# Rows of kv added by accumulating DMAs, and an order of work that knows of a port shared by VectorE and POOL

## The chip, the cores and the metric

The kernel runs on one core of one Trainium2 chip. Five engines work side by side on that core, each through its own instructions in a fixed order: TensorE (PE, with its weight loads PEld), VectorE (DVE), ScalarE (ACT), GpSimd (POOL) and SyncE (SP, which here only issues DMAs). POOL issues DMAs too. The metric is the time of one execution on the device, in microseconds (us). Three executions of the kernel before took 2118.57, 2122.62 and 2124.64 us, so the median is 2122.62 us.

## The reference

Two parts run one after the other. The first is attention over pooled keys: `kv` (4 batches, 384 x 32 x 128) is averaged over blocks of 4 x 4, multiplied by `w_sr`, and is both key and value for `q` (4 batches of 12288 rows of 128). The second is a mixture of 8 experts: each of the 49152 result rows goes to its best expert.

```python
kv_pool = kv.reshape(B, H // r, r, W // r, r, C).mean(axis=(2, 4))      # r = 4
k = v = kv_pool.reshape(B, -1, C) @ w_sr                                 # 768 keys per batch
a = softmax((q @ k.transpose(0, 2, 1)) / sqrt(C))
x = (a @ v).reshape(-1, C)
logits = (x / |x|) @ (emb / |emb|).T / tau ;  e = argmax(logits) ;  gate = softmax(logits)[e]
out = gate * (relu(x @ w1[e]) @ w2[e])                                   # F = 1024
```

Everything is float32 outside; the kernel splits its matmul operands into two float16 parts, a high one and a low one.

## The kernel before

The rows of `q` are cut into 96 steps of 512 rows, 24 to a batch. In a step, PE makes the scores `s` (four tiles of 128 x 768, line 668), DVE takes each row's maximum (`nm`, line 673), ACT makes the exponentials `p` (line 691) and their high half `phi` (line 709), DVE or POOL the low half `plo` (line 719), two DMA transposes turn both (line 743), and PE multiplies by the values (`xp`, line 764). POOL splits the result rows (`rows`, line 797) and scatters them to their experts' places in DRAM (line 188, one indirect DMA for 128 rows). A group of four steps has one router chain of small DVE instructions (tiles `n..z`, `y`, `x`, `d`, lines 823 to 960).

From step 23 on, tiles of 512 rows of one expert run between the steps: PE makes `ph` (line 1381), ACT `hh` (line 1388), DVE `hl` (line 1393), PE `po` (line 1417), DVE `o` (line 1427), and POOL scatters it to the output (line 188). After the last step expert tiles run alone.

The pooled keys of batch 0 are made at the start by DVE. Those of batches 1 to 3 are made while the batch before runs, in eight parts of 512 columns. For each part SP loads two tiles `kvt` with two of the four rows each (line 365; two buffers, 384 KB each). POOL adds each pair of rows (line 374), adds the two sums (line 378), and then adds the columns four to one in two instructions, `kvc` (line 390) and `pooled` (line 395). Later PE turns `pooled` (`pp`, line 353), and the keys `k` follow.

The order on each engine is worked out when the kernel is built. Every piece of work is recorded with `add(engine, duration, key, function, *what it waits for)`, and `Plan.run` replays the recording against an assumed clock: the engine that is free first takes, of its pieces that are ready by then, the one with the lowest key. The function is called at that moment, so the instructions of an engine stand in the order in which the plan started them. On the chip each engine runs its own list in that order and waits where a semaphore says so. A piece that is planned at the wrong moment therefore holds up all that stands behind it on its engine. The plan knows engines, DMAs and PSUM banks, and no other resource.

Lines that the change touches: `Op`, `Plan.add`, `Plan.chain` and `Plan.run` (202 to 335), `kv_load`, `kv_rows` and `kv_cols` (361 to 400), `kv_ops` (1502 to 1565), and the places where DVE and POOL work is recorded (1606 to 1791).

Of the kernel before, what the change touches and what calls it, by code (L numbers as in the profile page):

```python
# [51 lines left out]
def attention_moe(  # L52
# [149 lines left out]
    class Op:  # L202


        def __init__(self, eng, dur, key, fn, deps, dma, take, free, hold, lands, stage):
            self.eng, self.dur, self.key, self.fn, self.dma = eng, dur, key, fn, dma
            self.take, self.free, self.lands, self.stage = take, free, lands, stage
            self.left, self.users, self.ready, self.end = 0, [], 0.0, None
            if hold:
                self.ready = key + X["start"] - X["early"]  # L210
            for d in set(deps):
                if d is not None:
                    self.left += 1
                    d.users.append(self)

    class Plan:
# [8 lines left out]
        def add(self, eng, dur, key, fn, *deps, dma=None, take=None, free=None, hold=False, lands=False):  # L225
            op = Op(eng, dur, key, fn, deps, dma, take, free, hold, lands, self.stage)
# [3 lines left out]
        def chain(self, key, step, fns, *deps, dur=0.17, eng="DVE"):  # L230

            ops = []
            for i, fn in enumerate(fns):
                ops.append(self.add(eng, dur, key + i * step, fn, *(deps if not ops else ops[-1:])))
# [15 lines left out]
        def run(self, begin):  # L250

            soon, now, free = {}, {}, {}
            n = stage = 0
# [14 lines left out]
            while any(count):  # L268
# [92 lines left out]
    def kv_load(b, h, i):  # L361
# [4 lines left out]
        st[b]["kvt", h, i] = t  # L366

    def kv_rows(b, h, eng):


        def half(i):
            t = st[b].pop(("kvt", h, i))
            st[b]["r", h, i] = kvs.tile([NI, QC], F32, tag=f"kva{i}", name=f"kva{b}_{h}_{i}", bufs=2)
            eng.tensor_tensor(out=st[b]["r", h, i], in0=t[:, 0, :], in1=t[:, 1, :], op=ALU.add)

        def both():
            r = st[b]["r", h, 0]
            eng.tensor_tensor(out=r, in0=r, in1=st[b].pop(("r", h, 1)), op=ALU.add)

        return [lambda: half(0), lambda: half(1), both]  # L380

    def kv_cols(b, h, eng):


        def third():
            if h == 0:
                st[b]["pooled"] = kvs.tile([NI, NJ, C], F32, tag="pooled", name=f"pooled{b}")
            v = st[b].pop(("r", h, 0)).rearrange("p (j r c) -> p j r c", j=JQ, r=R)
            a3 = kvs.tile([NI, JQ, 2, C], F32, tag="kva3", name=f"kvc{b}_{h}", bufs=2)
            eng.tensor_tensor(out=a3, in0=v[:, :, 0:2, :], in1=v[:, :, 2:4, :], op=ALU.add)  # L390
            st[b]["a", h] = a3

        def fourth():
            a3 = st[b].pop(("a", h))
            eng.tensor_tensor(
                out=st[b]["pooled"][:, h * JQ : (h + 1) * JQ, :], in0=a3[:, :, 0, :], in1=a3[:, :, 1, :],
# [1077 lines left out]
    def kv_rows_0():  # L1474
# [3 lines left out]
        for h in range(NQR // 2):  # L1478
            t0, acc = -46.0 + 4 * h, []
            for i in range(R):  # L1480
# [3 lines left out]
                else:  # L1484
                    if h == 0 and i == R - 1:
                        x_set = setup(-30.0, x_wsr, x_tau, x_emb, acc[-1])
                    acc.append(add("DVE", 1.1, t0 + 1.0 + i, lambda h=h, i=i: kv_sum_0(h, i), first, o, *acc[-1:]))
# [14 lines left out]
    def kv_ops(b):  # L1502
        mine = [None] * NQR
        for h in range(NQR if b else 0):
            t0 = slot(b * SPB, -8 * (X["kv"] - h * X["kvs"]))
            eng, what, ta, tb_ = nc.gpsimd, "POOL", 1.25, 0.7
            rows = kv_rows(b, h, eng)
            parts = []
            for i in range(2):
                o = add("SP", 0.45, t0 + i, lambda h=h, i=i: kv_load(b, h, i), *turn("kvt", 2), dma=1.3, hold=True)  # L1510
# [392 lines left out]
```

## Time and profile before

| | us | share of the span |
|---|---|---|
| median of three executions | 2122.62 | |
| profiled execution, its own time | 2131.34 | |
| its span, first to last instruction | 2129.6 | 100% |
| PE busy | 1953.8 | 92% |
| DVE busy | 1740.2 | 82% |
| ACT busy | 1550.0 | 73% |
| POOL busy | 1329.7 | 62% |

The profiled execution took 8.7 us longer than the median of the other three. Busy time is the time in which an engine had an instruction running; an instruction that has started and is held up inside counts as busy. "Idle" before an instruction is what the engine stood still, with what ended it. The granted TensorE clock is given as a share of full speed (2.4 GHz), and was 0.982 on the mean of the span.

### The profile page before, as it was taken

Reading aid. Unit: us, or ns where it says so; the run is one execution under the profiler, and the core shown is the slowest. Engines: PE = TensorE matmul, PEld = TensorE weight load, DVE = VectorE, ACT = ScalarE, POOL = GpSimd, SP = SyncE. Lnnn points to the kernel's source line nnn. Section 1 sums busy time; section 2 is a strip of 40 time slices with the busy share of each in tenths; the row PEclk is TensorE's granted clock in tenths of the full one; section 3 lists DMA queues with packets and bytes.
Section 4 is the critical chain, followed back from the end, with each engine's and each line's share of the span. In section 5 each row is a group of like instructions: output and inputs, shape, how many; then the busy total and the mean of one; then the engine's idle time right before and its main releaser. Section 6 shows DMA issues by size and latency. Waiting matters only on the chain. (4 is left out here: it accounts for less than half of the span.)

```text
span 2129.6 us, 57497 instructions
## 1 busy us (share of the span) xinstructions
PE 1953.8 (92%) x21396; PEld 1498.0 (70%) x21396; DVE 1740.2 (82%) x3679; ACT 1550.0 (73%) x3256; POOL 1329.7 (62%) x1824
## 2 busy tenths in 40 slices
PE   3787788899989999899999999999999999999998
PEld 1575666677767767677677777777777777777697
DVE  6899788788898897788888888888888888766565
ACT  3888779778767777677777887888888887744443
POOL 1556765377768668477676576566566567567433
PEclk9999999999999999999999999999999999999999
DMA  8897646999879989879887888988888887623242
GB/s 234 195 219 179 170 97 143 170 178 181 163 139 177 163 161 182 175 135 181 156 163 141 148 158 153 198 146 159 149 164 150 149 148 151 116 62 80 57 92 77
DMA packets 844925, 322.64 MB, mean 151 GB/s; under 512 B 793042, under 2 KB 804443, under 8 KB 842848
## 3 DMA queue, kind: packets, MB, share of 16 engines
q1 hardware_dynamic: 817568, 264.13, 66.5%
q0 software_dynamic: 24704, 53.53, 9.6%
q8 instruction: 170, 2.79, 0.5%
q10 hardware_dynamic: 2368, 1.25, 0.2%
q14 instruction: 115, 0.94, 0.1%
HBM read 170.55 MB, written 64.50 MB: 110 GB/s over the span
## 5 line engine op out<-in xcount | busy, mean ns | idle before, releaser
L1393 DVE SCALAR_TENSOR_TENSOR hl<-ph,hh 128x512 f16<-128x512 f32 x740 | 506.7, 685 | 171.2 <-ACT hh L1388 163.9
L1381 PE MATMUL ph<-x,wbuf 128*128 128x512 f16 (+1 forms) x2328 | 606.0, 372 | 24.0 <-DVE hl L1393 23.2
L188 POOL DMA_INDIRECT out_dram<-o,m x388 | 409.0, 1054 | 326.5 <-DVE o L1427 97.7
L1388 ACT ACTIVATE hh<-ph 128x512 f16<-128x512 f32 x740 | 440.7, 596 | 229.6 <-PE ph L1381 176.4
L188 POOL DMA_INDIRECT xs_rows<-rows,pi x384 | 418.7, 1090 | 130.2 <-issue 112.1
L1417 PE MATMUL po<-wbuf,hh 128*128 128x128 f16 x5920 | 453.9, 220 | 34.3 <-ACT hh L1388 22.2
L668 PE MATMUL s<-k,qT 128*128 128x512 f16 (+1 forms) x2304 | 439.6, 330 | 20.3 <-ACT p L691 12.1
L691 ACT ACTIVATE p<-s,nm,qa 128x768 f32<-128x768 f32 x384 | 380.8, 993 | 106.3 <-DVE nm L685 90.3
L1417 PEld LDWEIGHTS <-hh 128*128 128x128 f16 x6208 | 384.0, 98 | 57.1 <-ACT hh L1388 26.5
L719 DVE TENSOR_TENSOR plo<-p,phi 128x768 f16<-128x768 f32 x339 | 344.0, 1016 | 55.0 <-ACT phi L709 45.7
L673 DVE TENSOR_REDUCE nm<-s 128x1 f32<-128x768 f32 x384 | 364.1, 949 | 12.8 <-PE s L668 9.6
L1381 PEld LDWEIGHTS <-wbuf 128*128 128x128 f16 x2544 | 227.1, 98 | 143.3 <-issue 31.1
L668 PEld LDWEIGHTS <-qT 128*128 128x128 f16 x2304 | 217.9, 99 | 149.8 <-issue 30.0
L764 PE MATMUL xp<-v,pthi 128*128 128x137 f16 x4200 | 313.8, 224 | 10.0 <-DVE w L551 4.3
L764 PEld LDWEIGHTS <-pthi 128*128 128x128 f16 x4200 | 275.7, 98 | 48.2 <-issue 13.8
L1417 PEld LDWEIGHTS <-hl 128*128 128x128 f16 x3104 | 230.3, 98 | 112.3 <-issue 3.5
L709 ACT CAST phi<-p 128x768 f16<-128x768 f32 x345 | 287.4, 834 | 11.6 <-DMA pthi<-phi 7.0
L1417 PE MATMUL po<-wbuf,hl 128*128 128x128 f16 x2960 | 287.5, 220 | 0.0
L764 PE MATMUL xp<-v,ptlo 128*128 128x137 f16 x2100 | 188.4, 225 | 2.7 <-DMA ptlo<-plo 2.7
L764 PEld LDWEIGHTS <-ptlo 128*128 128x128 f16 x2100 | 143.0, 98 | 3.2 <-DMA ptlo<-plo 3.2
L797 POOL TENSOR_TENSOR rows<-x,rows 128x512 f16<-128x512 f32 x96 | 114.7, 1195 | 30.2 <-ACT rows L792 29.9
L683 ACT ACTIVATE nm<-nm,scales,qa 128x1 f32<-128x1 f32 x206 | 79.4, 385 | 74.0 <-DVE nm L673 72.3
(359 smaller groups left out, 2042.8 us busy)
## 6 DMA issues: line engine op xcount, KB each, us to landing
wbuf<-w_prep SPq DMA_DIRECT2D x106, 1026.0 KB
kvt<-in_kv_dram SPq DMA_DIRECT2D x64, 384.0 KB
q<-in_q_dram SPq DMA_DIRECT2D x96, 256.0 KB
wf<-in_moe_w_dram SPq DMA_DIRECT2D x16, 512.0 KB
out_dram<-o,m POOLq DMA_INDIRECT x388
xs_rows<-rows,pi POOLq DMA_INDIRECT x384
w_prep<-wo SPq DMA_DIRECT2D x8, 514.0 KB
w_prep<-wo SPq DMA_DIRECT2D x8, 512.0 KB
```

Source lines behind the costliest of these rows:

```text
L188: ins = nc.gpsimd.indirect_dma_start(out=dst[:, :], out_offset=bass.IndirectOffsetOnAxis(ap=idx, axis=0), in_=src, in_offset=None, bounds_ ...
L668: nc.tensor.matmul(t[:, lo:hi], qs[:, l, :], r[:, lo:hi], start=i == 0, stop=i == 2)
L673: V.tensor_reduce(out=nm, in_=ks[k]["s", j], axis=AX.X, op=ALU.max, negate=True)
L691: nc.scalar.activation(out=p, in_=ks[k].pop(("s", j)), func=AF.Exp, bias=ks[k].pop(("nm", j)), scale=ks[k]["fac"],)
L709: nc.scalar.copy(out=hi, in_=p)
L719: eng.tensor_tensor(out=lo, in0=ks[k].pop(("p", j)), in1=hi, op=ALU.subtract)
L764: nc.tensor.matmul(ks[k]["xp", h][:, i, :w], l[:, c, :], r[:, c, :w], start=n == 0, stop=n == len(terms) - 1)
L797: nc.gpsimd.tensor_tensor(out=r[:, :, HP : HP + C], in0=ks[k]["x"][:, :, 0:C], in1=r[:, :, 0:C], op=ALU.subtract)
L1381: nc.tensor.matmul(ph[:, kk * n : (kk + 1) * n], wt[:, o + f : o + f + P], r, start=i == 0, stop=i == 2)
L1388: nc.scalar.activation(out=hh, in_=ts[t]["ph", u], func=AF.Relu)
L1393: V.scalar_tensor_tensor(out=hl, in0=ts[t].pop(("ph", u)), scalar=0.0, in1=ts[t]["hh", u], op0=ALU.max, op1=ALU.subtract)
L1417: nc.tensor.matmul(ts[t]["po"][:, j * C : (j + 1) * C], h[:, kk * n + j * P : kk * n + (j + 1) * P], wt[:, f : f + P], start=u == 0 and i ...
```

## The change

Batches 1 to 3 get their rows of `kv` added by DMA. A tile `kva` now holds 1024 columns (four parts to a batch and four buffers). SP loads the first of the four rows, and POOL issues three DMAs that each add the next row onto the tile, each of which waits until the one before it has landed (`lands=True`, and the chain through `o`). POOL then adds the columns in two instructions, in place and without `kvc`. So a batch has 4 loads and 12 accumulating DMAs where it had 16 loads, and 8 POOL additions where it had 40.

Second, a piece of work can be marked `port=True`. `Plan.run` keeps the time until which DVE and POOL each hold the port by its own reckoning. Where a marked piece would start while the other engine still holds it, the engine takes the lowest-keyed unmarked piece that is ready instead, and where there is none, the piece is reckoned to start when the other engine lets go. Marked are DVE's `plo`, `q_lo`, `w_lo`, the low half of `k`, the router chain and one of the placing steps, and POOL's `rows`, `w_lo`, `plo`, column additions and selection of tiles. The instructions of these pieces stay what they were; the recorded duration of a router step goes from 0.17 to 0.22.

```diff
+            held = dict(DVE=0.0, POOL=0.0)
...
+                if op.port:
+                    other = held["POOL" if eng == "DVE" else "DVE"]
+                    if other > t + 0.1:
+                        rest = [x for x in now[eng] if not x[2].port and self.can_go(x[2])]
+                        if rest:
+                            x = min(rest)
+                            now[eng].remove(x)
+                            now[eng].append((op.key, i, op))
+                            heapq.heapify(now[eng])
+                            op = x[2]
+                        else:
+                            t = other
+                if op.port:
+                    held[eng] = t + op.dur
                 op.end = t + op.dur
...
-        t = kvs.tile([NI, 2, QC], F32, tag="kvt", name=f"kvt{b}_{h}_{i}", bufs=2)
-        src = kv[b].rearrange("(i r) w c -> i r (w c)", r=R)
-        nc.sync.dma_start(out=t, in_=src[:, 2 * i : 2 * i + 2, h * QC : (h + 1) * QC])
...
+    def kv_load(b, h):
+
+        st[b]["r", h] = kvs.tile([NI, 2 * QC], F32, tag="kva", name=f"kva{b}_{h}", bufs=NQR // 2)
+        nc.sync.dma_start(out=st[b]["r", h], in_=kv_src(b, h, 0))
+
+    def kv_add(b, h, i):
+        nc.gpsimd.dma_start(out=st[b]["r", h], in_=kv_src(b, h, i), accum_op=ALU.add)
...
+            eng.tensor_tensor(out=v[0][:, :, 0:2, :], in0=v[0][:, :, 0:2, :], in1=v[0][:, :, 2:4, :], op=ALU.add)
...
+                out=st[b]["pooled"][:, h * 2 * JQ : (h + 1) * 2 * JQ, :], in0=v[0][:, :, 0, :], in1=v[0][:, :, 1, :],
                 op=ALU.add,
...
+            t0 = slot(b * SPB, -8 * (X["kv"] - 2 * h * X["kvs"]))
+            o = took("kva", add("SP", 0.45, t0, lambda h=h: kv_load(b, h), *turn("kva", NQR // 2), dma=1.3, hold=True))
+            for i in range(1, R):
+                o = add("POOL", 1.1, t0 + 4.0 * i, lambda h=h, i=i: kv_add(b, h, i), o, dma=2.0, lands=True)
+            cols = kv_cols(b, h, nc.gpsimd)
+            r = add("POOL", 1.25, t0 + 16.0, cols[0], o, *(turn("pooled", 1) if h == 0 else mine[h - 1 : h]), port=True)
...
+            mine[h] = add("POOL", 0.85, t0 + 16.4, cols[1], r, port=True)
...
                             ENG[on[1]], P_LO[on[1]], v + i + 0.5, lambda j=j, i=i: p_lo(k, j - 1 + i), his[i],
-                            *(los if i else turn("plo", 2)),
+                            *(los if i else turn("plo", 2)), port=True,
```

Two places show what that does to the lists. The first is POOL's list in the middle of batch 1, where the rows for batch 2 are added (`kva2_h` is part h of batch 2). Before:

```order
L378 TENSOR_TENSOR kva2_2_0_8461<-kva2_2_0_8461,kva2_2_1_8492 96x512
L188 DMA out_0_dram<-o10_9524,m10_8169 49152x128 x4
L390 TENSOR_TENSOR kvc2_2_9664<-kva2_2_0_8461 96x256
L374 TENSOR_TENSOR kva2_3_0_9692<-kvt2_3_0_8520 96x512
L395 TENSOR_TENSOR pooled2_6862<-kvc2_2_9664 96x128
L374 TENSOR_TENSOR kva2_3_1_9722<-kvt2_3_1_8923 96x512
L807 COPY x8_9364<-x32_9538 128x32
L378 TENSOR_TENSOR kva2_3_0_9692<-kva2_3_0_9692,kva2_3_1_9722 96x512
L797 TENSOR_TENSOR rows0_116<-x32_9538,rows0_116 128x4x128
```

And now, at the place where parts 0 to 3 of batch 2 are under way:

```order
L386 DMA kva2_0_5329<-in_kv_dram 96x1024
L802 TENSOR_TENSOR rows0_116<-x24_6099,rows0_116 128x4x128
L805 IOTA rows0_116 128x4
L188 DMA out_0_dram<-o3_6524,m3_5253 49152x128 x4
L397 TENSOR_TENSOR kva2_0_5329<-kva2_0_5329 96x2x256
L386 DMA kva2_1_5334<-in_kv_dram 96x1024
L400 TENSOR_TENSOR pooled2_6677<-kva2_0_5329 96x256
L386 DMA kva2_2_6288<-in_kv_dram 96x1024
L386 DMA kva2_3_6310<-in_kv_dram 96x1024
L386 DMA kva2_1_5334<-in_kv_dram 96x1024
```

Four additions in a row stood between the scatters; now there are DMA issues with one or two additions among them, and the second and third addition onto `kva2_1` stand four rows apart.

The second place is DVE's list in the router chain of group 7 (`n7z`, `y7`), with `hl11_3` the low half of unit 3 of expert tile 11, and `plo34_0` that of step 34. Before:

```order
L835 TENSOR_TENSOR n7z_9536<-y7_7838 128x16
L719 TENSOR_TENSOR plo34_0_9512<-p34_1_9510,phi34_0_9460 128x768
L838 SCALAR_TENSOR_TENSOR n7z_9536<-n7z_9536,ss7_7837 128x16
L1393 SCALAR_TENSOR_TENSOR hl11_3_9625<-ph11_3_9577,hh11_3_9603 128x512
L841 SCALAR_TENSOR_TENSOR y7_7838<-n7z_9536,y7_7838 128x16
```

And now:

```order
L840 TENSOR_TENSOR n7z_9715<-y7_7777 128x16
L843 SCALAR_TENSOR_TENSOR n7z_9715<-n7z_9715,ss7_7776 128x16
L678 TENSOR_REDUCE nm35_1_9752<-s_1_160 128x1
L846 SCALAR_TENSOR_TENSOR y7_7777<-n7z_9715,y7_7777 128x16
L1398 SCALAR_TENSOR_TENSOR hl12_1_9801<-ph12_1_9745,hh12_1_9779 128x512
```

The chain of group 7 stands beside step 35 and expert tile 12 where it stood beside step 34 and tile 11, about a step later, and no `plo` lies in this piece of it.

## Rows read from the trace of the kernel before

**Rows 1.** The head of the profile's page and its first part: busy time of each engine, share of the span, number of instructions.
```profile
span 2129.6 us, 57497 instructions
PE 1953.8 (92%) x21396; PEld 1498.0 (70%) x21396; DVE 1740.2 (82%) x3679; ACT 1550.0 (73%) x3256; POOL 1329.7 (62%) x1824
```

**Rows 2.** Busy time by stretch: from and to in us, length, then busy time (and number of instructions) of PE, PEld, DVE, ACT and POOL, the granted clock, the DMA engines' share and GB/s. Six stretches of nearly equal work in which POOL adds rows of kv (one of them shown, and the sum over the six), and then three of the same work in which it does not (one shown, and the sum).
```profile
558.00:645.00 87.00, 78.59 (x868) 58.50 (x866) 76.01 (x149) 63.55 (x137) 64.04 (x88) 0.98 0.85 160
...
sum 501.00, PE 464.54 PEld 350.49 DVE 435.05 ACT 376.56 POOL 360.28; mean PE 77.42 PEld 58.42 DVE 72.51 ACT 62.76 POOL 60.05
...
1153.00:1230.00 77.00, 76.11 (x870) 57.77 (x868) 66.78 (x147) 61.80 (x133) 49.31 (x76) 1.00 0.86 153
...
sum 230.00, PE 227.31 PEld 172.71 DVE 200.00 ACT 186.15 POOL 147.99; mean PE 75.77 PEld 57.57 DVE 66.67 ACT 62.05 POOL 49.33
```

**Rows 3.** Timeline of POOL and DVE around 613 us: start in us, duration, engine, line, operation.
```profile
613.42 0.74 POOL L390 TENSOR_TENSOR kvc<-kva 96x256 f32<-96x256 f32 x1
613.43 4.40 DVE L719 TENSOR_TENSOR plo<-p,phi 128x768 f16<-128x768 f32 x1
614.10 1.28 POOL L374 TENSOR_TENSOR kva<-kvt 96x512 f32<-96x512 f32 x1
615.32 0.47 POOL L395 TENSOR_TENSOR pooled<-kvc 96x128 f32<-96x128 f32 x1
615.74 1.26 POOL L374 TENSOR_TENSOR kva<-kvt 96x512 f32<-96x512 f32 x1
```

**Rows 4.** Who waited for whom between 612 and 626 us: us in total, times, longest. Then all executions on DVE of the lines of `plo` and of `hl`: duration in ns, shortest, median and longest.
```profile
ACT nm L683 <- DVE nm L673: 4.3, 1, 4.3
PE ph L1381 <- DVE hl L1393: 2.5, 2, 2.0
PE po L1417 <- ACT hh L1388: 1.6, 1, 1.6
...
L719 DVE TENSOR_TENSOR plo<-p,phi x339: 935/954/4397, 60.4 to 1848.2; 128x768 f16<-128x768 f32 x170
...
L1393 DVE SCALAR_TENSOR_TENSOR hl<-ph,hh x740: 621/686/693, 369.7 to 2118.3; 128x512 f16<-128x512 f32 x185
```

**Rows 5.** POOL's additions and its issues of DMAs, all executions: duration in ns, shortest, median and longest, first and last start.
```profile
L374 POOL TENSOR_TENSOR kva<-kvt x48: 1252/1264/1758, 126.8 to 1127.0; 96x512 f32<-96x512 f32 x48
L378 POOL TENSOR_TENSOR kva<-kva,kva x24: 1253/1266/1879, 130.6 to 1128.4; 96x512 f32<-96x512 f32 x24
L390 POOL TENSOR_TENSOR kvc<-kva x24: 719/724/1462, 132.0 to 1131.9; 96x256 f32<-96x256 f32 x24
L395 POOL TENSOR_TENSOR pooled<-kvc x24: 447/454/1052, 132.8 to 1132.8; 96x128 f32<-96x128 f32 x24
...
L188 POOL DMA_INDIRECT xs_rows<-rows,pi x384: 966/1008/1951, 157.9 to 1968.8; - x192
```

**Rows 6.** The page's group for the last of these: busy time in us, mean ns of one, idle time before them and what ended it.
```profile
L188 POOL DMA_INDIRECT xs_rows<-rows,pi x384 | 418.7, 1090 | 130.2 <-issue 112.1
```

**Rows 7.** POOL's time in the instructions that write or read `kva` (lines 374, 378 and 390), by stretch: the sums over the six stretches of rows 2, over three stretches from 100 to 280 us, and over three from 382 to 477 and 809 to 984 us. The last row is the time of line 395 over the whole span.
```profile
sum 501.00, POOL 55.71; mean POOL 9.28
...
sum 180.00, POOL 37.08; mean POOL 12.36
...
sum 270.00, POOL 20.78; mean POOL 6.93
...
sum 2130.00, POOL 12.06; mean POOL 12.06
```

**Rows 8.** Stretches of four steps each before the expert tiles begin, columns as in rows 2: three with additions of kv, and two without.
```profile
100.00:150.00 50.00, 42.72 (x397) 34.71 (x396) 44.78 (x98) 42.51 (x93) 29.13 (x29) 0.97 0.94 217
150.00:205.00 55.00, 44.29 (x380) 35.35 (x381) 49.91 (x109) 44.53 (x95) 38.86 (x41) 0.94 0.75 191
205.00:280.00 75.00, 55.89 (x451) 44.88 (x449) 61.81 (x129) 52.88 (x111) 49.44 (x51) 0.91 0.58 143
...
280.00:330.00 50.00, 44.71 (x401) 36.07 (x400) 41.20 (x103) 42.32 (x93) 31.78 (x54) 1.00 0.55 114
330.00:382.00 52.00, 46.56 (x430) 35.22 (x428) 45.64 (x113) 44.53 (x88) 27.83 (x51) 1.00 0.79 161
```

**Rows 9.** The same view of the two stretches in which the keys of batches 2 and 3 are made, and of the saturated stretch before the last steps end.
```profile
809.00:911.00 102.00, 92.62 (x997) 68.64 (x995) 77.54 (x175) 73.12 (x158) 65.29 (x96) 0.95 0.91 177
1307.00:1398.00 91.00, 88.61 (x1002) 66.86 (x1000) 77.27 (x171) 72.44 (x158) 57.24 (x89) 1.00 0.91 182
...
1544.00:1900.00 356.00, 352.50 (x4068) 268.90 (x4067) 291.85 (x635) 270.80 (x585) 235.44 (x342) 1.00 0.76 138
```

**Rows 10.** Timeline of SP and POOL around 207 us: a pair of kv loads is issued, and the addition that waits for it starts (in brackets the idle time before it and what ended it). Then who waited in SP's queue for POOL to free a `kvt` buffer, in the whole span.
```profile
207.29 1.30 SPq L365 DMA_DIRECT2D kvt<-in_kv_dram  x2
...
212.11 1.27 POOL L374 TENSOR_TENSOR kva<-kvt 96x512 f32<-96x512 f32 x1 [4.18 <-DMA kvt<-in_kv_dram]
...
SPq L365 <- POOL kva L374: 8.1, 6, 2.4
```

**Rows 11.** Timelines of POOL and PE in batch 1: the last part of `pooled` for batch 2 is finished, and PE turns the first of it.
```profile
773.91 0.48 POOL L395 TENSOR_TENSOR pooled<-kvc 96x128 f32<-96x128 f32 x1
...
891.68 0.50 PE L353 MATMUL pp<-ident,pooled 96*128 96x96 f32 x4
```

More of the change, by code (lines that the diff above doesn't have):

```diff
@@ L223, in __init__, with add, chain @@
             self.moved, self.stage, self.late, self.giving = 0.0, 0, False, False
-        def add(self, eng, dur, key, fn, *deps, dma=None, take=None, free=None, hold=False, lands=False):
-            op = Op(eng, dur, key, fn, deps, dma, take, free, hold, lands, self.stage)
+        def add(self, eng, dur, key, fn, *deps, dma=None, take=None, free=None, hold=False, lands=False, port=False):
+            op = Op(eng, dur, key, fn, deps, dma, take, free, hold, lands, port, self.stage)
             self.ops.append(op)
             return op
-        def chain(self, key, step, fns, *deps, dur=0.17, eng="DVE"):
+        def chain(self, key, step, fns, *deps, dur=0.17, eng="DVE", port=False):
             ops = []
             for i, fn in enumerate(fns):
-                ops.append(self.add(eng, dur, key + i * step, fn, *(deps if not ops else ops[-1:])))
+                ops.append(self.add(eng, dur, key + i * step, fn, *(deps if not ops else ops[-1:]), port=port))
             return ops
@@ L359, in attention_moe, with kv_src @@
     st = [dict() for _ in range(B)]
-    def kv_load(b, h, i):
-        t = kvs.tile([NI, 2, QC], F32, tag="kvt", name=f"kvt{b}_{h}_{i}", bufs=2)
-        src = kv[b].rearrange("(i r) w c -> i r (w c)", r=R)
-        nc.sync.dma_start(out=t, in_=src[:, 2 * i : 2 * i + 2, h * QC : (h + 1) * QC])
[L366 to L380, printed above, removed]
+    def kv_src(b, h, i):
+        return kv[b].rearrange("(i r) w c -> i r (w c)", r=R)[:, i, h * 2 * QC : (h + 1) * 2 * QC]
+    def kv_load(b, h):
[3 more added lines that the diff above has]
+        nc.gpsimd.dma_start(out=st[b]["r", h], in_=kv_src(b, h, i), accum_op=ALU.add)
     def kv_cols(b, h, eng):
+        v = []
         def third():
@@ L1486, in kv_rows_0 @@
                         x_set = setup(-30.0, x_wsr, x_tau, x_emb, acc[-1])
-                    acc.append(add("DVE", 1.1, t0 + 1.0 + i, lambda h=h, i=i: kv_sum_0(h, i), first, o, *acc[-1:]))
+                    acc.append(add("DVE", 1.1, t0 + 1.0 + i, lambda h=h, i=i: kv_sum_0(h, i), first, o, *acc[-1:], port=True))
                     reads("kvt0", acc[-1])
@@ L1502, in kv_ops @@
     def kv_ops(b):
[L1503 to L1510, printed above, removed]
-                took("kvt", o)
-                r = took(f"kva{i}", add(what, ta, t0 + 8.0 + i * 0.1, rows[i], o, *parts, *turn(f"kva{i}", 2)))
-                reads("kvt", r)
-                parts.append(r)
-            r = add(what, ta, t0 + 8.2, rows[2], *parts)
-            reads("kva1", r)
-            cols = kv_cols(b, h, eng)
-            r = add(what, tb_, t0 + 8.3, cols[0], r, *(turn("pooled", 1) if h == 0 else mine[h - 1 : h]))
+        mine = [None] * (NQR // 2)
+        for h in range(NQR // 2 if b else 0):
+            t0 = slot(b * SPB, -8 * (X["kv"] - 2 * h * X["kvs"]))
[4 more added lines that the diff above has]
+            r = add("POOL", 1.25, t0 + 16.0, cols[0], o, *(turn("pooled", 1) if h == 0 else mine[h - 1 : h]), port=True)
             if h == 0:
                 took("pooled", r)
-            reads("kva0", r)
-            mine[h] = add(what, 0.45, t0 + 8.4, cols[1], r)
+            mine[h] = add("POOL", 0.85, t0 + 16.4, cols[1], r, port=True)
+            reads("kva", r, mine[h])
         copies = []
@@ L1560, in kv_ops @@
         hi = add("ACT", 0.83, key, lambda: kv_k_hi(b), sc)
-        lo = add("DVE", 0.93, key, lambda: kv_k_lo(b), hi)
+        lo = add("DVE", 0.93, key, lambda: kv_k_lo(b), hi, port=b > 0)
         if b:
@@ L1611, in w_ops @@
                     took("wo0", o)
-                o = add(ENG[eng[2]], 1.2 if eng == " AD" else 2.1, v, lambda e=e, i=i: w_lo(e, i), o)
+                o = add(ENG[eng[2]], 1.2 if eng == " AD" else 2.1, v, lambda e=e, i=i: w_lo(e, i), o, port=True)
                 scaled.setdefault(e, []).append(o)
@@ L1649, in step_ops @@
             hi = took("q2", add("ACT", 0.61, key, lambda: q_hi(k), qa, *turn("q2", 2)))
-            lo = add("DVE", 0.66, key + 0.5, lambda: q_lo(k), hi)
+            lo = add("DVE", 0.66, key + 0.5, lambda: q_lo(k), hi, port=True)
             uses["q"][k % 2 - 2].append(lo)
@@ L1773, in group_ops @@
             deps = pc[-1:] if i else [rk, *chosen.get(g - 5, ())]
-            pc.append(add("DVE", 0.22, t + 0.3 * i, fn, *deps, free=f"rk{g}" if i == 1 else None))
+            pc.append(add("DVE", 0.22, t + 0.3 * i, fn, *deps, free=f"rk{g}" if i == 1 else None, port=i == 2))
         gc = chain(t + 0.5, 0.3, gates, ex, pc[-1], dur=0.15)
```

22 lines of the change are left out of this document (10 added, 12 removed).

## The prediction

> **What bounds the kernel now.** The page's head comes first: PE is busy 92% of the span and DVE 82% [rows 1]. Were that even, a DVE made faster would be hidden behind PE. So the second view is busy time by stretch, over stretches of nearly the same work that differ in whether POOL adds rows of kv [rows 2]. Six with such additions take 501 us, 83.5 each; three without take 230 us, 76.67 each. PE has 501 - 464.54 = 36.5 us of idle time in the six and 230 - 227.31 = 2.7 in the three; DVE is busy 72.51 us a stretch against 66.67. The excess is 501 - 6 x 76.67 = 41 us, of which 6 x 5.84 = 35 also show as DVE time. Before the expert tiles start it is the same: 180 us for three stretches where two without kv take 50 and 52, so 180 - 3 x 51 = 27 us too long [rows 8].
>
> The third view, the timeline, says how. At 613 us one `plo` is on DVE for 4.40 us, while POOL runs four additions from 613.42 to 617.0 [rows 3]; its median is 0.954 [rows 4]. So a DVE instruction that reads SBUF twice is held up while POOL adds. What that does to the others stands in the waits of the next 14 us: ACT waits 4.3 us for a maximum behind this `plo`, PE 2.5 us for `hl` and 1.6 for ACT [rows 4]. So it reaches PE, but not in full: of about 3.4 us too many, PE shows 2.5 to 4.1. And where POOL doesn't add, PE bounds: 352.5 of 356 us from 1544 on [rows 9], 227.3 of 230 above.
>
> **Part 1, POOL's additions.** Before, 48 + 24 row additions at about 1.265 us, 24 of `kvc` at 0.724 and 24 of `pooled` at 0.454 [rows 5] make 91.1 + 17.4 + 10.9 = 119 us by medians, 125.6 as measured (55.71 + 37.08 + 20.78 for the first three lines, 12.06 for `pooled` [rows 7]). After, 12 instructions that write 96x512 and 12 that write 96x256 remain, priced by [rows 5] at 1.264 and 0.724: 23.9 us. So 81% of the time in which POOL can hold DVE goes.
>
> The most this can give in the six stretches is 41 x 0.81 = 33 us. I take 0.6 of it, 20 us, since the DVE time itself (35 of the 41) is fully explained by the additions, while the granted clock there (0.98 against 1.00, PE busy 77.42 against 75.77) and what DVE does next need not follow. From 100 to 280 us the most is 27 x 0.81 = 22; I take 0.4, 9 us, because these stretches also have the start-up and the clock down to 0.91 [rows 8], which the additions needn't have caused. In 382 to 477 and 809 to 984 us another 20.78 us of these lines run [rows 7]; at the six's rate (41 / 55.71 = 0.74 of excess for each us) the most is 20.78 x 0.74 x 0.81 = 12. I take 4: the stretch in which the keys of batch 2 are made takes 102 us and its like for batch 3 takes 91 [rows 9], but it has few of these additions, so most of those 11 us come from something else. Part 1: -33, with bounds of 0 and -67.
>
> **Part 2, the accumulating DMAs.** 36 are issued by POOL. The nearest rows are its indirect DMAs, 1.09 us each on the mean [rows 6]: 36 x 1.09 = 39 us. POOL's work thus falls by 125.6 - 23.9 - 39 = 63 us. POOL was busy 60.05 us of 83.5 in the six stretches [rows 2], so the issue time itself is covered by POOL's idle time.
>
> In the trace, 384 issues of `xs_rows`, beside a DVE busy 82%, took 1.008 us at the median, 1.09 on the mean and 1.951 at most [rows 5, 6], so a busy DVE lengthens few of them, and I keep 39 us. The Trainium skill's page "SBUF — State Buffer" (section "Summary: rules for kernel authors") speaks against the edit: the descriptors of a DMA issued by POOL are starved while DVE runs in its 2x or 4x modes. If by that rule each of the 36 took the longest time of rows 5, POOL would lose 36 x (1.951 - 1.09) = 31 us more, of which its busy share of 72% would not be hidden, and the sum would end at -28 + 22 = -6, 2117 us.
>
> Each accumulation waits until the one before has landed. No row shows an accumulating DMA; the nearest is a kv load, issued at 207.29 and used at 212.11, 4.8 us [rows 10]. The list now has two accumulations onto `kva2_1` four rows apart, with one addition and two issues between: 0.72 + 2 x 1.05 = 2.8 us, so POOL stands 2 us at such a place. In the list there are few; with 12 of 36 so close it is 24 us, in which POOL's idle time (28% there) hides most. I take +3. That nothing waits for the end of kv is in [rows 11]: `pooled` for batch 2 is done at 773.9 and PE turns it at 891.7, 118 us later. The bytes read from DRAM stay the same; each accumulation also reads its tile. The DMA engines are 85% busy there [rows 2], and a load of two rows of the same size was 4.8 us. I take +2 for later transposes. SP issues 12 loads instead of 48, and its 8.1 us of waiting for `kvt` goes [rows 10]; that lay in SP's queue ahead of transposes, and I give it nothing. Part 2: +5. Below, -2 (SP's queue freer); above, +90, the second rival.
>
> **Part 3, the order.** Marked pieces are the same instructions at other places. DVE's list is shifted by some five instructions on the whole and by some 20 in the first fifth, PE's hardly. Gain: where `plo` no longer starts under POOL's `rows`, some of DVE's remaining excess goes too. Loss: `plo` stands behind one more DVE piece, and the transposes, which need it, are later. Neither shows in a row, so I bound it by the cases: -10 (a quarter of the excess that part 1 leaves, 41 + 27 - 20 - 9 = 39), and +49, the third rival. I take 0, as saturated stretches are bound by PE whichever way DVE's list goes [rows 9].
>
> Sum: -20 - 9 - 4 + 3 + 2 + 0 = -28. The profiled execution took 2131.34 us with a span of 2129.6, so a profiled one of the new kernel takes about 2103; it stands 8.7 above the median of three, and taken off that median, -28 gives 2122.62 - 28 = 2095 us.
>
> **The rivals.** No change: DVE's time was hidden and the six stretches are long for other reasons, such as the clock. For it speaks PE's 92% and the 11 us of the keys' stretches that the additions don't explain; against it that three stretches of the same work with PE at 99% differ in just this. Result 2122, give or take 6.
>
> Slower by late landings: on the chip an accumulation takes 12 us or more until it has landed, since it must read, add and write each element. POOL then stands blocked before each of 36, and `rows`, scatters and x copies queue behind. 36 x 12 + 39 - 102 = 369 us more of POOL, against some 28% of idle time over about 1000 us (126.8 to 1132.8 [rows 5]), 280 us: about 90 appear, less part 1's 33: 2180. It decides from 10.4 us of landing (36 x 10.4 + 39 - 102 = 311, which is 280 and 31). Against it: 4.8 us for a plain load, and most steps of the chains stand more than four rows apart.
>
> Slower by the order: the reckoned port pushes `plo` behind other DVE work. If in each of the 72 steps of batches 1 to 3 one `hl` (0.686 us [rows 4]) thus comes between and the transposes are later by it, that is 72 x 0.69 = +49, less 28: 2144. It decides from 28 / 72 = 0.4 us a step. For it: ACT already waits for DVE (4.3 us at 613). Against it: PE is so near its limit from 1544 on that buffers there must hide more than that.
>
> The whole excess goes: the upper ends 33 + 22 + 12 = 67 with no cost: 2056. For it speaks that PE's clock is 1.00 wherever PE isn't held up [rows 2, 8]; against it the unexplained 11 us and the 19% of additions left.
>
> **How the numbers follow.** The forecast (2080 to 2112 by itself) has 0.58; no change 0.10; late landings 0.05; order 0.12; whole excess 0.15. The range of 2062 to 2134 leaves out the lower half of the whole excess, late landings and most of the order case, two in ten. 0.3% (6.4 us) is about what a measurement of this kernel can tell from no change. Faster by more: 0.58 + 0.15 = 0.73, and 0.01 of the order case at its mild end, 0.74. Within: 0.10. Slower: 0.05 + 0.11 = 0.16.
>
> **What would show it.** Right: POOL's additions take 20 to 28 us in all, an 83.5 us stretch of rows 2 falls to about 80, DVE's mean there from 72.5 to about 68, no `plo` of 4 us stands under POOL additions, and PE's idle time in the six falls by half. The accumulations' issues take about 1.1 us, and POOL's waits for their landing sum to under 30 us. Wrong, if these stretches keep their length with DVE freed (no change), if POOL's waits for landings sum to over 200 us (late landings), or if PE's and ACT's waits for `plo`, `hl` and the transposes grow from 1544 on, where no kv is added (order). I am also wrong if the gain comes outside 100 to 1153 us.

## The result, and the profile after

The kernel after took 2130.78 us (median of 13 runs, 2123.39 to 2147.39), the kernel before 2120.55 (13 runs beside them). The ratio is 1.0052, with a 95% interval of 1.0038 to 1.0066: slower by half a per cent, where 2095 was forecast. The profiled execution spans 2133.1 us. The head and the first part of its page:

```profile
span 2133.1 us, 57336 instructions
PE 1948.4 (91%) x21396; PEld 1501.3 (70%) x21396; DVE 1693.2 (79%) x3679; ACT 1550.4 (73%) x3256; POOL 1255.2 (59%) x1764
```

Against [rows 1], DVE is busy 47 us less and POOL 75 us less, so the work went away as forecast. The time didn't. Busy time by stretch, PE alone (from and to, length, PE busy and instructions, granted clock, share of the DMA engines, GB/s), first of the kernel before, then of the kernel after:

```profile
130.00:185.00 55.00, 47.28 (x447) 1.00 0.77 189
185.00:280.00 95.00, 69.83 (x553) 0.89 0.62 155
280.00:477.00 197.00, 175.79 (x1739) 0.98 0.79 155
477.00:558.00 81.00, 75.64 (x855) 0.98 0.89 167
558.00:1153.00 595.00, 551.28 (x6098) 0.98 0.87 162
```

```profile
130.00:185.00 55.00, 27.89 (x223) 0.83 1.12 144
185.00:280.00 95.00, 83.66 (x763) 0.97 0.79 171
280.00:477.00 197.00, 159.66 (x1420) 0.92 0.74 146
477.00:558.00 81.00, 72.86 (x796) 0.96 1.12 173
558.00:1153.00 595.00, 577.65 (x6538) 0.99 0.95 168
```

PE has the same work in both, so a stretch with more busy time and more instructions is one in which it got more done. (Once a kernel is late a stretch holds other steps; by steps it is read under the experiments.) From 558 to 1153 us the kernel after gains 26.4 us. Before 558 it loses 19.4, 16.1 and 2.8 in three stretches and gains 13.8 in one. The loss starts where the twelve accumulating DMAs of batch 1 are issued (135 to 183 us): PE is busy 28 of 55 us, while the DMA engines are busy all the time (the share adds the packets of two queues, so it can pass 1) and move only 144 GB/s. Who waited between 140 and 190 us (us in total, times, longest):

```profile
ACT pw L740 <- PE s L369: 21.1, 1, 21.1
PEld L769 <- DMA ptlo<-plo: 19.8, 1, 19.8
PE xp L769 <- DMA ptlo<-plo: 19.6, 1, 19.6
DVE plo L724 <- DMA ptlo<-plo: 18.3, 1, 18.3
POOL kva L397 <- DMA kva<-in_kv_dram: 14.5, 1, 14.5
POOL kva L386 <- DMA kva<-in_kv_dram: 12.9, 5, 3.9
```

PE, DVE and with them ACT wait for one transpose of `plo`. SP's timeline says why it is late (start, duration of the issue):

```profile
142.54 2.94 SPq L748 DMA_TRANSPOSE pthi<-phi  x1
148.53 12.96 SPq L748 DMA_TRANSPOSE ptlo<-plo  x1
161.58 19.97 SPq L748 DMA_TRANSPOSE pthi<-phi  x1
181.64 6.31 SPq L748 DMA_TRANSPOSE ptlo<-plo  x1
```

Four transposes take 42 us to issue, where the median of one is 1.5 to 1.8 us. Whether the bytes, the second queue or the kind of packet holds them up is what the first two experiments ask.

In four stretches like those of [rows 2], with hardly an addition and two accumulating DMAs in them, the kernel after needs 76.5 us each in place of 83.5, and DVE is busy 67.39 in place of 72.51. The other two, in which more of these DMAs stand, take 84.0 and 79.6. The four:

```profile
594.00:670.00 76.00, 75.44 (x865) 57.48 (x863) 68.71 (x152) 63.39 (x140) 49.66 (x73) 1.00 0.98 170
...
sum 306.00, PE 302.41 PEld 230.50 DVE 269.57 ACT 253.19 POOL 201.00; mean PE 75.60 PEld 57.63 DVE 67.39 ACT 63.30 POOL 50.25
```

### The profile page after: what moved, and what is told of

Read it like the earlier page. It is cut to its first block, busy times and chain, and to the rows that moved or that the text cites. A ratio compares the mean times of both kernels' runs of the same rounds, so it can differ in the third digit from the quotient of the medians.

```text
span 2133.1 us, 57336 instructions
## 1 busy us (share of the span) xinstructions
PE 1948.4 (91%) x21396; PEld 1501.3 (70%) x21396; DVE 1693.2 (79%) x3679; ACT 1550.4 (73%) x3256; POOL 1255.2 (59%) x1764
## 4 chain that ended last, share of the span: by engine, by line
PE 58%; DVE 11%; DMA 9%; ACT 7%; issue 5%; POOL 4%; SPq 0%; POOLq 0%; DVEq 0%; ACTq 0%
PE po L1422 17%; PE ph L1386 16%; PE xp L769 11%; PE s L673 9%; DMA ptlo<-plo 4%; DVE nm L678 3%; DMA qT<-q 2%; POOL xs_rows L188 2%; ACT p L696 2%; DVE plo L724 2%; DVE hl L1398 2%; PE xp L761 2%; ACT hh L1393 1%; DMA kva<-in_kv_dram 1%; PE s L1386 1%
## 5 line engine op out<-in xcount | busy, mean ns | idle before, releaser
L1386 PE MATMUL ph<-x,wbuf 128*128 128x512 f16 (+1 forms) x2328 | 604.7, 372 | 15.0 <-DVE hl L1398 14.2
L724 DVE TENSOR_TENSOR plo<-p,phi 128x768 f16<-128x768 f32 x339 | 337.5, 997 | 57.1 <-DMA ptlo<-plo 40.1
L769 PEld LDWEIGHTS <-pthi 128*128 128x128 f16 x4200 | 277.9, 99 | 52.7 <-issue 19.4
L769 PE MATMUL xp<-v,ptlo 128*128 128x137 f16 x2100 | 190.4, 227 | 24.5 <-DMA ptlo<-plo 24.5
L817 ACT ACTIVATE junk<-x 128x128 f32<-128x128 f32 x384 | 116.6, 312 | 6.9 <-DVE x L790 6.9
```

What stands on the lines that cost most here:

```text
L724: eng.tensor_tensor(out=lo, in0=ks[k].pop(("p", j)), in1=hi, op=ALU.subtract)
L769: nc.tensor.matmul(ks[k]["xp", h][:, i, :w], l[:, c, :], r[:, c, :w], start=n == 0, stop=n == len(terms) - 1)
L817: nc.scalar.activation(out=junk, in_=ks[k]["x"][:, j, 0:C], func=AF.Square, accum_out=groups[g]["ss"][:, i * NQ + j : i * NQ + j + 1],)
L1386: nc.tensor.matmul(ph[:, kk * n : (kk + 1) * n], wt[:, o + f : o + f + P], r, start=i == 0, stop=i == 2)
```

## The experiments

The first four ran on a chip like that of the prediction (the kernel before took 2122.75 us beside them). All later ones fell on other chips, on which the kernel before takes 2339 to 2390 us; those are read as ratios to the kernel before beside them.

**The accumulating DMAs left out.**

```diff
-        nc.gpsimd.dma_start(out=st[b]["r", h], in_=kv_src(b, h, i), accum_op=ALU.add)
+        pass
```

> The kernel after, with the 36 accumulating DMAs left out (rows 1 to 3 of kv are not added for batches 1 to 3); the order of all other instructions is the same as in the kernel after. Theory DMA (the accumulating DMAs share the DMA engines with the transposes, and those of batch 1, twelve between 135 and 163 us, hold them up): the stall of PE between 160 and 185 us (20.0 us idle there, 3.9 before) goes, no transpose takes SP over 6 us to issue, and the time falls by 20 to 45 us, to 2086 to 2111. Rival ORDER (the new order of the lists costs the time): the time stays at 2122 to 2137, and PE's idle time from 280 to 510 us stays 15 to 20 us above the kernel before.

It took 2072.05 us, ratio 0.9774 (0.9739 to 0.9809): 59 us below the kernel after, past the range of theory DMA. PE is busy 47.84 of 55 us from 130 to 185 and 587.70 of 595 from 558 to 1153. ORDER falls: the same lists, without 36 DMAs, are 48 us faster than the kernel before. That is not what the additions cost, since the kernel before moves those rows too.

**Plain DMAs in their place.**

```diff
-        nc.gpsimd.dma_start(out=st[b]["r", h], in_=kv_src(b, h, i), accum_op=ALU.add)
+        nc.gpsimd.dma_start(out=st[b]["r", h], in_=kv_src(b, h, i))
```

> The kernel after, with each of the 36 DMAs on POOL's queue writing its row over the tile in place of adding it (so the sum is left out); the order is the same, each DMA still waits for the one before. Theory QUEUE (what costs is a second queue that shares the DMA engines packet by packet with SP's transposes): the stall near 160 to 185 us stays at two thirds or more, the time 2118 to 2137. Rival ADD (what costs is that an accumulating packet takes longer, 0.43 us on the mean for 4096 bytes where others of that size take 0.25): the stall falls to less than half, packets take about 0.25 us, and the time is 2095 to 2115. Rival ORDER: no change, 2125 to 2137, with the stall gone.

It took 2083.21 us, ratio 0.9814 (0.9789 to 0.984). So of the 59 us, 48 are those of accumulating (by the ratios, 50). The other 11 (by the ratios, 8) are those of moving the bytes on POOL's queue; they are not firm, since the intervals of the two kernels overlap. QUEUE falls, ADD stands; the time is even below the range that ADD expected. PE by stretch, to be set against the kernel after:

```profile
130.00:185.00 55.00, 45.01 (x364) 0.94 1.03 221
185.00:280.00 95.00, 79.01 (x656) 0.95 0.57 144
280.00:477.00 197.00, 171.81 (x1684) 0.96 0.81 164
477.00:558.00 81.00, 80.22 (x908) 1.00 1.01 183
558.00:1153.00 595.00, 581.97 (x6632) 1.00 0.93 169
```

In the first stretch accumulating takes 17.1 us of PE's work. Later the stretches of the two kernels hold different steps, so the price is read from the start of each step (its first maximum `nm` on DVE; one profiled execution each, us):

| | step 8 | step 12 | step 24 | step 32 | step 60 | span |
|---|---|---|---|---|---|---|
| before | 150.2 | 208.7 | 388.6 | 559.7 | 1153.8 | 2129.6 |
| after | 155.4 | 235.2 | 429.6 | 595.2 | 1153.3 | 2133.1 |
| plain DMAs | 150.5 | 212.2 | 403.9 | 554.0 | 1103.5 | 2081.8 |
| left out | 148.1 | 206.0 | 400.2 | 550.6 | 1093.1 | 2069.1 |

The kernel after is 5 us behind the one with plain DMAs at step 8, and was so at step 4, before the first of these DMAs. Then it loses 18 us to step 12 (batch 1's DMAs), 3 to step 24, 15 to step 32 (batch 2's), 9 to step 60 (batch 3's) and 1.5 to the end. So the stall is less than half of the price. From step 12 to 24 all three kernels with the new lists take 192 to 194 us, where the kernel before takes 180, whatever their DMAs do.

What waits for the transposes shows the path: their issues (ns: shortest, median, longest) and who waited for them (us, times), in the kernel after and then with plain DMAs:

```profile
L748 SPq DMA_TRANSPOSE pthi<-phi x175: 1280/1478/19973, 62.2 to 1848.7; - x175
L748 SPq DMA_TRANSPOSE ptlo<-plo x175: 1280/1842/12955, 63.8 to 1855.1; - x175
...
  DVE plo L724: 40.1, 8
...
  PE xp L769: 24.5, 3
```

```profile
L748 SPq DMA_TRANSPOSE pthi<-phi x175: 1277/1488/8631, 59.5 to 1798.7; - x175
L748 SPq DMA_TRANSPOSE ptlo<-plo x175: 1280/1816/4972, 61.2 to 1805.8; - x175
...
  DVE plo L724: 14.0, 6
...
  PE xp L769: 5.1, 3
```

PE itself waits 19.4 us less, DVE 26.1 less. In the kernel before PE waited 3.7 us for them and DVE 5.5. How much of DVE's waits reaches PE isn't shown. The page's DMA part has the price in the engines: packets, MB and share of 16 engines of POOL's queue, in the kernel after, with plain DMAs, and with none:

```profile
q0 software_dynamic: 28736, 67.69, 14.0%
```

```profile
q0 software_dynamic: 28736, 67.69, 12.4%
```

```profile
q0 software_dynamic: 24704, 53.53, 9.7%
```

Times the spans (2133.1, 2081.8 and 2069.1 us) these are 299, 258 and 201 us of all sixteen engines. The same 14.16 MB cost 57 us as plain DMAs and 98 us as accumulating ones, 1.6 against 2.7 us for each of 36. How that meets the transposes is seen from 148 to 163 us; the packets on q1 there are transposes alone (about 250 bytes each). The kernel after, and then the one with plain DMAs:

```profile
q0 software_dynamic: 501, 1.77, 78.0%
q1 hardware_dynamic: 1199, 0.30, 38.9%
```

```profile
q0 software_dynamic: 448, 1.57, 58.9%
q1 hardware_dynamic: 4071, 1.03, 56.3%
```

Beside about as many packets of POOL's queue, 1199 transposing packets were moved in 15 us in place of 4071. One of them took 0.389 x 240 / 1199 = 78 ns beside accumulating packets, 33 beside plain ones. (The DMA engines of the plain kernel are nearly as busy from 130 to 185 us, 1.03 against 1.12, so a high share alone doesn't hold the transposes.) POOL pays too: an issue took 941 ns at the median and 554 when plain, 14 us for all 36, and no run separates that from the 48 (shortest, median, longest; first the kernel after):

```profile
L386 POOL DMA_DIRECT2D kva<-in_kv_dram x36: 782/941/1470, 135.1 to 980.0; - x36
```

```profile
L386 POOL DMA_DIRECT2D kva<-in_kv_dram x36: 505/554/756, 130.3 to 931.7; - x36
```

**The accumulating DMAs without the rule on the port, and the rule without the DMAs.** The first sets the rule's two conditions to false and a router step back to 0.17; the second takes the kernel before, adds the rule, and marks all its POOL additions beside the pieces that the change marks.

```diff
-                if op.port:
+                if False:
                     other = held["POOL" if eng == "DVE" else "DVE"]
```

> The kernel after without the rule on the port (no piece gives way or waits, a router step is reckoned at 0.17 again): the accumulating DMAs alone. Theory DMA: the stall behind the twelve DMAs of batch 1 stays, the stretches from 558 to 1153 us stay fast, and the time is 2115 to 2140. Rival ORDER (the rule on the port is what costs): the time is 2090 to 2110, and PE's idle time from 280 to 510 us returns to within 5 us of the kernel before.

> The kernel before with the rule on the port alone: the rows of kv are added by POOL as before, all these additions marked, and the other pieces marked as in the kernel after. Theory DMA: the order costs little, 2105 to 2128, and DVE's additional time under POOL's additions (about 60 us before) falls. Rival ORDER: slower by 10 us or more, 2132 or above, with PE idle 10 us or more longer between 280 and 510 us than before.

They took 2129.47 us (1.0039, 1.0008 to 1.007) and 2118.34 (0.9978, 0.9958 to 0.9997). ORDER's times fall in both, and DMA has the times right, though ORDER's signs for PE from 280 to 510 us nearly come true: it is busy 209.1 us there without the rule (208.8 before, 190.9 in the kernel after) and 199.8 with the rule alone. Taking the rule away from the kernel after changes nothing that can be told; the rule alone gives at most 0.4%. But it moves time between stretches. PE from 280 to 477 and from 558 to 1153 us, without the rule, and then with the rule alone:

```profile
280.00:477.00 197.00, 179.48 (x1769) 0.99 0.79 160
...
558.00:1153.00 595.00, 560.59 (x6243) 0.97 0.94 163
```

```profile
280.00:477.00 197.00, 167.91 (x1564) 0.95 0.70 144
...
558.00:1153.00 595.00, 572.76 (x6456) 0.99 0.91 169
```

With POOL's additions kept, the rule brings 21.5 us from 558 to 1153 (551.28 before), and loses 7.9 from 280 to 477 (175.79 before). Without the rule nothing is lost from 280 to 477, so the 16.1 us that the kernel after loses there need the rule (with the rule and plain DMAs 4.0 are lost). In the late stretch the additions gone and the DMAs in their place bring 9.3. That run also has the price of accumulating in it, so 9.3 is a lower bound for the additions. The expectation that the late stretches stay fast without the rule was wrong where accumulating DMAs stand: there four steps take up to 88 us. Where neither DMAs nor additions stand (steps 36 to 40 and 56 to 60) they take 76.7 and 76.4, against 82.7 and 85.0 before. These two stretches without the rule, and then all six of [rows 2] (by steps) with the rule alone and every addition kept:

```profile
sum 153.10, PE 151.99 PEld 115.74 DVE 130.62 ACT 126.65 POOL 99.11; mean PE 75.99 PEld 57.87 DVE 65.31 ACT 63.33 POOL 49.56
```

```profile
sum 466.50, PE 453.11 PEld 344.52 DVE 419.44 ACT 376.18 POOL 358.08; mean PE 75.52 PEld 57.42 DVE 69.91 ACT 62.70 POOL 59.68
```

So the excess of these stretches goes without the additions, and with the rule it goes nearly as far (77.8 us in place of 83.5) although POOL adds as much as before. The two gains don't add up. DVE's time falls with the rule alone too, as was expected (69.91 in place of 72.51, and no `plo` over 3.2 us). Of the 35 us that the rule gains there 25 are lost again from step 8 to 28, which takes 353 us in place of 328.

**Do the data matter? Does spreading help?** Kernels that leave DMAs out have other keys and so other experts, which could change the time. One kernel adds row 0 three times (same lists, same traffic). Another holds the DMAs back in the plan, a third leaves out batch 1's alone.

```diff
-                o = add("POOL", 1.1, t0 + 4.0 * i, lambda h=h, i=i: kv_add(b, h, i), o, dma=2.0, lands=True)
+                ti = 130.0 + 12.0 * (3 * h + i - 1) if b == 1 else t0 + 6.0 * i
+                o = add("POOL", 1.1, ti, lambda h=h, i=i: kv_add(b, h, i), o, dma=2.0, hold=True, lands=True)
```

> The kernel after, in which all three accumulating DMAs of a part add row 0 again in place of rows 1 to 3 (so the keys of batches 1 to 3 are others, and with them the experts that the rows go to); order and traffic are the same. It checks whether the gain of the kernels with DMAs left out or made plain came from other data. Theory DMA: data don't matter, 2123 to 2147. Rival DATA: the time falls to 2100 or less.

> The kernel after, with the accumulating DMAs held back in the plan: for batch 1 they are planned 12 us apart, for batches 2 and 3 6 us apart within a part; bytes and count are the same. Theory BURST (an accumulating DMA costs little by itself, and what costs is that several in a row leave the transposes no room): the stall of 20 us goes, and the time is 2085 to 2115. Rival BYTES (each accumulating DMA costs its 1.3 us wherever it stands, 48 us in all for 36): the time stays at 2122 to 2140.

> The kernel after with the 12 accumulating DMAs of batch 1 left out (its rows 1 to 3 are not added), those of batches 2 and 3 kept; the order is the same. Theory BURST: batch 1's twelve, which stand in 28 us, cost more than a third of the 59 us that leaving all 36 out gave: 2095 to 2108. Rival BYTES: a third, 2108 to 2116. If they cost nothing, 2125 or more.

The kernel after had not run on such a chip, so all three were run again beside it:

> The kernel after itself, beside the next three on one chip. On the chip of the last three runs the kernel before took 2373 us, so those times can't be set against 2131. All theories: 1.002 to 1.008 times the kernel before where that takes about 2121 us; on a chip like the last, 0.97 to 0.99, as the row-0 kernel there.

> The kernel after, adding row 0 three times (other data, same order and traffic). Theory DMA: within 0.5% of the kernel after of this call. Rival DATA: 1.5% or more below it.

> The kernel after with the accumulating DMAs held back in the plan. Theory BURST: 20 to 45 us below the kernel after of this call, without its stall of 20 us between 160 and 185 us. Rival BYTES: within 8 us of it, or above.

> The kernel after with the 12 accumulating DMAs of batch 1 left out. Theory BURST: 23 to 36 us below the kernel after of this call. Rival BYTES: 15 to 22 us below. If they cost nothing, within 8 us.

| | ratio to the kernel before, first time | second time |
|---|---|---|
| after | | 0.9808 (0.9727 to 0.9889) |
| row 0 three times | 0.9796 (0.9677 to 0.9914) | 0.9786 (0.9718 to 0.9854) |
| held back in the plan | 0.9831 (0.9739 to 0.9924) | 0.9812 (0.9738 to 0.9887) |
| batch 1's left out | 0.9655 (0.9565 to 0.9745) | 0.9663 (0.9597 to 0.9729) |

Other data change nothing that the intervals show. Batch 1's twelve cost 1.45% of 2371 us, 34 us with the moving of their bytes, on these chips, which is what BURST had said. Held back in the plan, they gave nothing: the stall went (41.18 us of PE work from 130 to 185, against 27.89), but the lists of all engines changed with it, and PE's sum to 1900 us is the same, 1647.73 against 1648.35. So this kernel doesn't tell bursts from bytes.

**One accumulating DMA a step, all other lists kept.** Here the plan runs as in the kernel after, and a piece of the kv work is put into POOL's list only behind the next step's `rows`; PE, DVE, ACT and SP keep their lists word for word.

```diff
+        t = st[b]["r", h]
+        go = lambda: nc.gpsimd.dma_start(out=t, in_=kv_src(b, h, i), accum_op=ALU.add)
+        pend.append((True, go)) if b > 0 else go()
...
+        some()
```

> The kernel after with the accumulating DMAs of all three batches and the column additions behind them moved in POOL's list alone: each step's splitting of rows releases one of them, so they stand some 13 to 20 us apart. The lists of PE, DVE, ACT and SP are the same as in the kernel after, and so are bytes and count. Theory BURST: PE's stall between 160 and 185 us goes, no transpose takes SP over 8 us to issue, and the time is 25 to 50 us below the kernel after (2081 to 2106 where the kernel before takes about 2121). Rival BYTES: within 8 us of the kernel after.

> The same for batch 1 alone; batches 2 and 3 as in the kernel after. Theory BURST: 12 to 30 us below the kernel after (2101 to 2119), the rest of the gain of the run before being that of batches 2 and 3. Rival BYTES: within 8 us of the kernel after.

> The kernel after with the 12 accumulating DMAs of batch 1 left out, again, since it has not run on a chip where the kernel before takes about 2121 us. Theory BURST: 20 to 36 us below the kernel after, and no more than 12 us below the run in which batch 1's are one a step. Rival BYTES: 15 to 22 us below.

> The kernel after, adding row 0 three times (other data, same order and traffic). If the data don't matter, 2120 to 2147 where the kernel before takes about 2121 us; if the kernels that leave DMAs out owe their gain to other data, 2100 or less.

> The kernel with one accumulating DMA a step, again, for a chip on which the kernel before takes about 2121 us. On the chip with 2352 us it was 0.975 of the kernel before, against 0.981 for the kernel after on the same kind of chip, and kept 14 of the 33 us that leaving batch 1's DMAs out gave there. Theory BURST: 2085 to 2110 on a chip with 2121 us. Rival BYTES: 2122 to 2139. In between (2110 to 2122), both are at work.

One a step gave 0.9749 (0.9684 to 0.9814) and, again, 0.9747 (0.968 to 0.9815); for batch 1 alone 0.9753 (0.9701 to 0.9806); batch 1's left out 0.9675; row 0 three times 0.9848. With all three batches spread the gain is 14 us, which neither theory had; for batch 1 alone it is 13, BURST's mild end, but leaving batch 1's out gains 18 more where BURST allowed 12. SP's transposes flow (the longest takes 6.0 us to issue) and POOL waits 11.6 us for landings in place of 62.5 in the kernel after on such a chip. PE from 130 to 280 us, in the kernel after on such a chip and then with one a step:

```profile
130.00:185.00 55.00, 27.89 (x190) 0.75 1.14 129
185.00:280.00 95.00, 76.34 (x640) 0.93 0.69 163
```

```profile
130.00:185.00 55.00, 44.80 (x378) 1.00 0.78 182
185.00:280.00 95.00, 75.08 (x620) 0.93 0.69 152
```

PE has 15.7 us more work done by 280 us, and keeps about 0.6% (14 us) at the end, of the 34 that batch 1's DMAs cost there; the intervals of 0.975 and 0.981 overlap, so this size is not firm. That the burst makes the stall is shown. That bursts are the whole price is not: one a step stays 1.3% (31 us) above the kernel with plain DMAs (0.9618, below), so most of the price stays without the stall. It isn't shown that it stays wherever they stand: in the trace the spread DMAs of batch 1 are 2 to 49 us apart, so that some still stand two or three together.

**Plain DMAs again, and a trace of the kernel before on the slower chips.**

> The kernel with plain DMAs on POOL's queue in place of the accumulating ones, again. Where the kernel before takes about 2355 us the kernel after is 0.981 of it and the one with one a step 0.975. Theory ADD (the price is that of accumulating): 0.945 to 0.965 there, as 0.981 less the 48 us (2%) between this kernel and the kernel after on the first chip. Rival QUEUE: 0.972 to 0.985, no better than one a step. Where the kernel before takes 2121 us: 0.979 to 0.985, as before.

> The kernel before itself, for a trace of it on the slower chip. If the slower chip's added time lies in waits that POOL's additions cause, PE's idle time there is longer than in the kernel after by 40 us, most of it between 477 and 1153 us, and the two are alike from 1544 on. If not, the difference is spread evenly.

Plain gave 0.9618 (0.9572 to 0.9664), 1.9% or 45 us below the kernel after's 0.9808: the price of accumulating is that of the first chip (48). The trace of the kernel before (2349.02 us) doesn't fit its first guess. PE from 1544 to 1900 us, where no kv is added, in the kernel before and in the kernel after (on another of the slower chips):

```profile
1544.00:1900.00 356.00, 319.05 (x3457) 0.96 0.73 132
```

```profile
1544.00:1900.00 356.00, 331.47 (x3667) 0.99 0.78 139
```

The kernel after gains 12.4 us in that stretch and 13.4 in the one before it (1153 to 1544), where nothing but the order differs. With plain DMAs, on the same chip as the kernel before and in the new order, PE is busy 333.28 us from 1544 to 1900, 14.2 more. So these traces put a good part of the gain on the slower chips (2%) down to the new order; the rule alone was not run there, so that isn't shown. Why these chips are slower was not tried; the granted clock is 0.964 in the kernel before there and 0.982 in the trace of the first chip.

## Why the prediction was wrong

**What bounds the kernel**: right. Where POOL's additions or their delays go, a stretch falls from 83.5 to 76.5 us and PE is the bound.

**Part 1 (-33)**: the mechanism was right, and the size about right. POOL's additions now take 16.2 + 10.2 = 26.4 us (24 expected), DVE's mean fell to 67.4 (68 expected), no `plo` takes over 2.6 us (4.4 before [rows 4]), and without the rule, too, stretches without additions take 76.4 and 76.7 us. On top of the rule, with the same bytes moved (on POOL's queue in place of SP's), the additions gone give 1.64% (0.9814 with plain DMAs against 0.9978 with the rule alone): 35 us. What they give without the rule stays open, since a kernel with plain DMAs and no rule was not run.

**Part 2 (+5)**: wrong, and this is the step that failed. "I take +3" for POOL's waits and "I take +2 for later transposes" stand against 48 us by the medians, 50 by the ratios, for accumulating in place of plain DMAs. The nearest row, a kv load that landed in 4.8 us [rows 10], was a plain DMA, and nothing in the trace showed an accumulating one. The step asked what POOL waits for and where the path to `pooled` ends. Its waits for landings were put at under 30 us and sum to 43.1 + 22.5 = 66; that nobody needs `pooled` early was right. But POOL's waits aren't the price: with one DMA a step they fell to 11.6 us on the slower chips, and most of it stayed. The term that was mis-sized is, above all, that of the transposes. The step didn't ask what they lose to other packets in the same microseconds. The DMA engines were 94 and 75% busy in the first two stretches of [rows 8], accumulating made the same bytes cost 1.7 times the engine time, and the transposes, which PE needs within a step, share them: PE waited 24.5 us for them, and DVE 40.1. How the rest of the 48 reaches PE, through DVE's waits or POOL's longer issues, stays open.

The sum as measured, by ratios to the kernel before and with the same bytes in every kernel: -5 for the rule alone, -35 for the additions on top of it, +50 for accumulating, +10 or 11 in all.

**The issue price**: 36 x 0.97 = 35 us where 39 were put; right. The sentence drawn from the Trainium skill's page "SBUF — State Buffer" (section "Summary: rules for kernel authors"), that POOL's descriptors starve while DVE runs in its 2x or 4x modes, gave 2117 us and so came nearer by chance. The issues show no such time (1.47 us at most, where 1.951 was taken for each), and the transposes that wait are SP's.

**Part 3 (0)**: right as a sum (at most 0.4% alone), wrong as "nothing". The rule alone loses 8 us of PE's work from 280 to 477 us and brings 21 from 558 to 1153, on the first chip.

**The rivals**: late landings had the right culprit and the wrong victim. It let POOL stand blocked, from 10.4 us of landing on; POOL's longest wait was 14.5, its sum 66 us, and its busy share fell. The order rival forecast loss after 1544 us, where PE does 2.2 us more in the same time, not less; what the order costs, it costs from step 8 to 28. No change named a time near 2122, but its reason (the time of the additions hidden) is refuted by the kernel without DMAs. That the range of 2062 to 2134 held the measured 2130.78 was luck: nothing in the sum pointed there, and slower was given 0.16.

## What to carry to other kernels

Work that is taken off a compute engine and given to the DMA engines has to be priced there: bytes, the factor for the kind of transfer (accumulating took 1.7 times the engine time of plain here), and the share of those engines that is free in that stretch. Then ask which short transfer on the critical path shares them: here transposes that PE needs within a step were held 20 us by twelve large DMAs whose result PE took up only at 380 us. Leaving out the new transfers while keeping every list, and then making them plain, costs two runs and prices the kind of transfer; a third, with the same traffic and other data, shows that the wrong results of the two don't matter. Two remedies for one excess, such as the rule and the DMAs here, need a run each, since their gains may not add up.

## What the runs showed that was not expected

The price of accumulating was the same on chips of different speed (48 and 45 us), but the verdict was not: 1.0052 on one chip, 0.981 (0.973 to 0.989) on others, where by the traces the new order brought more (not tried alone there). The rule on the port alone, which moves no work, took 35 of the 41 us of excess out of the six stretches of [rows 2], and lost 25 before them. And a POOL issue of an accumulating DMA took 0.94 us where a plain one of the same shape took 0.55.
